# A new hand-out of work: the order table of an attention, DFT and FFN kernel drawn up again

## The chip, the cores and the metric

The kernel runs on one core of a Trainium2 chip. The metric is the device time of one execution in microseconds (us). The engines of the core are TensorE (PE: matmul, with PEld its weight loads), VectorE (DVE), ScalarE (ACT), GpSimd (POOL) and SyncE (SP), which here issues nearly all DMAs. Each engine works through its own list of instructions in order.

## What is computed

Batch 4, sequence 768, 8 heads of 48, so a model width of 384. A linear attention with decay, then a mixing by a two-dimensional DFT (the real part), a normalization, and an FFN of hidden width 1536 with ReLU:

```python
for t in range(S):
    cur = np.einsum('bhd,bhe->bhde', u[None] * kt, vt)
    y[:, :, t] = np.einsum('bhd,bhde->bhe', rt, state + cur)
    state = wt[:, :, :, None] * state + np.einsum('bhd,bhe->bhde', kt, vt)
...
X = np.fft.fft(x, axis=1)
X = np.fft.fft(X, axis=2)
u = x + np.real(X)
un = (u - mean(u)) / np.sqrt(var(u) + 1e-06)
out = u + np.maximum(un @ w_ch1, 0.0) @ w_ch2
```

Inputs and the output are float32.

## The kernel before

**Work.** The sequence of each batch is cut into six chunks of 128 tokens, 24 chunks in all, numbered n = 6 b + c. Names in the rows of the profile are those of the tiles.

*Attention* (`attention2` for pairs of chunks of batch 0, `attention` for the others). A chunk's r, k, v and w are loaded (`in_r` and so on, L587 or L596). ScalarE takes the logarithm of w (`lb`); TensorE sums it along the tokens (L944, L948); ScalarE turns the sums into decays (L950, L963, tile `e`). Products with them are `rkh`: its first half rh (L982, VectorE) and its second half kh (the helper line L533). `rk` is r times k, then times u; its reduction is `dc` (L971), and `vtd` is v times that. rh and kh are transposed to `rkt`: on TensorE for the chunks of batches 0 and 1, and by a DMA transpose (L990) for those of batches 2 and 3. L1014 multiplies the transposed halves, L1019 masks the product (`ah`), L1040 is the state, and L1061 and L1064 give the chunk's output, which L1070 writes to `x`.

*Folding and mixing.* `fold` adds and subtracts mirrored halves of x (`sd`, `xf`; even and odd parts). L1128 is the DFT along the tokens; its results are copied to `hcs`, and a mirrored copy of them to `hcr` (L537, L1138, L1142). L1151 is the DFT along the width; L1153 adds x (`uf`), L1157 and L1159 give mean and variance (`bst`, `agg`), and `un` is normalized up to a scale. `un` is transposed to `unt`: on TensorE (L1174) for batches 0 and 1, by a DMA transpose (L1180) for batches 2 and 3.

*FFN.* A batch is done in two halves of 384 tokens; q counts them from 0 to 7. FFN1 (L1198): twelve results per half, each three matmuls of 128x384, and each evicted with a ReLU from PSUM to `ht` by VectorE (L1203) or ScalarE (L1205). FFN2 (L1216): three blocks of 128 tokens per half. L1220 scales, adds uf (`osb`), and a DMA writes the block out (L1224). The FFN's two weights (`w`, W1 and W2, 1152 KB each) come by DMAs that GpSimd issues (L755).

**Order.** The functions record operations with what they read and write. Several can run on two or three engines: `vec` (L533) on GpSimd or VectorE, `evict` (L556, L557), the FFN1 evictions, `un` and `hcr` on ScalarE or others. `ORDER` (L34) then says everything: for each engine, the numbers of the operations that it does, in order. `schedule` goes through the five lists together. It gives each PSUM tile one of eight banks, in the order in which banks come free by its own planned times; a tile's first operation then depends on the last of the bank's former tile. It also adds one kind of dependence that the data don't ask for:

```python
                    p = port["pool"] if e == "dve" else ahead.end + self.LAT[e] if ahead else 0
...
                if e == "pool" and ahead:
                    o.deps.add(ahead)
            if o.port and e == "dve":
                ahead = o
```

A GpSimd operation that uses the shared port waits for the last such VectorE operation that stands ahead of it in the plan. `emit` turns dependences into semaphore waits, and each engine runs its list in order, so an instruction that waits holds up all that is behind it on its engine, on SyncE too.

Of the kernel before, what the change touches and what calls it, by code (L numbers as in the profile page):

```python
# [32 lines left out]

ORDER = {  # L34
# [24 lines left out]
    "act": (  # L59
# [12 lines left out]
    "dve": (  # L72
# [15 lines left out]
    "pool": (  # L88
# [12 lines left out]
}  # L101


class _Tile:


    __slots__ = ("bank", "ops", "pool", "n_done", "end")

# [1184 lines left out]
```

## Time and profile before

| | |
|---|---|
| Runs | median 183.23 us of 3 (182.76 to 184.08) |
| Profiled execution | 183.38 us, span 181.6 us |
| Outside the span | 1.8 us |
| Busy, us | PE 172.1, DVE 156.6, ACT 120.1, POOL 96.1 |
| Granted TensorE clock | 1.000 |
| First FFN1 matmul | 45.3 us in the chain of waits |
| Last FFN2 matmuls | end about 178.4; then `osb`, and the last output DMA |
| W1's issue | 34.27 us |

"Waited" in a row means that the engine stood idle until the named thing ended. A row of the chain of waits gives the start, the length and what it was; PE rows in it carry a line and how many pieces they hold. Matmuls overlap, so the mean time of one (326 ns for 128x384) is twice their spacing.

### The profile page before, as it was taken

How to read it: one execution, taken by the hardware profiler on the slowest of the kernel's cores; microseconds unless marked ns; L12 is line 12 of the kernel's file. 1: busy time of each engine (PE TensorE's matmuls, PEld its weight loads, DVE VectorE, ACT ScalarE, POOL GpSimd, SP SyncE). 2: the span in 40 equal slices, each digit the busy share in tenths (PEclk: the TensorE clock that was granted, in tenths of full speed). 3: DMA queues.
4: the chain of work that ended last, by engine and by line, in shares of the span. 5: the costliest groups of instructions: out<-in, count | busy, mean ns of one | idle time of the engine just before them, and what ended most of it. 6: DMA issues, size and time to landing. Idle time of an engine off the chain costs nothing.

```text
span 181.6 us, 4639 instructions
## 1 busy us (share of the span) xinstructions
PE 172.1 (95%) x1776; PEld 122.6 (67%) x1776; DVE 156.6 (86%) x372; ACT 120.1 (66%) x286; POOL 96.1 (53%) x121
## 2 busy tenths in 40 slices
PE   5798999999999999999999999997999999999992
PEld 2355577756888767667777776585776866877761
DVE  8999999999996998999999999999688979864233
ACT  4999999999988747678848796349394342415110
POOL 2136988499989806696698035946747230000000
PEclk9999999999999999999999999999999999999999
DMA  5999988999899889898898999999982104330043
GB/s 148 324 323 269 212 168 176 199 187 210 172 191 208 175 158 215 172 221 165 151 196 175 182 222 196 228 198 139 228 194 74 43 4 105 88 110 0 4 167 137
DMA packets 108935, 30.58 MB, mean 168 GB/s; under 512 B 105201, under 2 KB 108402, under 8 KB 108786
## 3 DMA queue, kind: packets, MB, share of 16 engines
q1 hardware_dynamic: 108370, 27.93, 71.8%
q0 software_dynamic: 544, 2.36, 6.9%
q8 instruction: 14, 0.23, 0.5%
q14 instruction: 7, 0.06, 0.1%
HBM read 23.59 MB, written 4.72 MB: 156 GB/s over the span
## 4 chain that ended last, share of the span: by engine, by line
PE 56%; DVE 17%; DMA 6%; SPq 6%; ACT 6%; POOL 5%; issue 2%; DVEq 0%; ACTq 0%; POOLq 0%
PE bank L1216 19%; PE bank L1198 18%; SPq L596 4%; PE bank L1151 4%; DMA rkt<-rkh 3%; PE bank L1128 2%; PE bank L1014 2%; DMA in_k<-in_k_dram 2%; DVE osb L1220 2%; DMA out_dram<-osb 2%; POOL rkh L533 2%; DVE bst L1157 2%; DVE uf L1153 2%; DVE ah L1019 1%; PE bank L839 1%
## 5 line engine op out<-in xcount | busy, mean ns | idle before, releaser
L1198 PE MATMUL bank<-unt,w 128*128 128x384 bf16 x288 | 54.8, 329 | 0.0
L1216 PE MATMUL bank<-w,ht 128*128 128x384 bf16 (+2 forms) x300 | 54.1, 320 | 0.0
L1205 ACT ACTIVATE ht<-bank 128x384 bf16<-128x384 f32 x77 | 35.6, 496 | 26.7 <-PE bank L1198 26.7
L1198 PEld LDWEIGHTS bank<-unt,w 128*128 128x128 bf16 x288 | 38.8, 144 | 6.4 <-DVE ht L1203 0.3
L1216 PEld LDWEIGHTS bank<-w,ht 128*128 128x128 bf16 x300 | 27.7, 98 | 16.0 <-DVE ah L1019 0.2
L1019 DVE TENSOR_TENSOR ah<-bank,msk 128x512 bf16<-128x512 f32 x36 | 23.7, 683 | 2.7 <-PE bank L1014 2.5
L533 POOL TENSOR_TENSOR vtd<-in_v,dc 128x384 f32<-128x384 f32 (+1 forms) x23 | 19.2, 844 | 8.7 <-DVE dc L971 4.8
L533 POOL TENSOR_TENSOR rk<-rk,ub 128x384 f32<-128x384 f32 x21 | 21.1, 1008 | 2.8 <-DVE rkh L533 2.4
L533 POOL TENSOR_TENSOR rkh<-in_k,e 128x384 bf16<-128x384 f32 x16 | 16.0, 1001 | 8.0 <-DMA in_k<-in_k_dram 3.9
L1220 DVE SCALAR_TENSOR_TENSOR osb<-bank,rstd,uf 128x384 f32<-128x384 f32 (+2 forms) x25 | 14.4, 592 | 5.0 <-PE bank L1216 4.5
L533 POOL TENSOR_TENSOR rk<-in_r,in_k 128x384 f32<-128x384 f32 x16 | 16.2, 1019 | 3.5 <-DVE agg L1159 1.7
L1203 DVE TENSOR_SCALAR ht<-bank 128x384 bf16<-128x384 f32 x19 | 10.1, 552 | 7.3 <-PE bank L1198 7.2
L950 ACT ACTIVATE bank<-bank 128x384 f32<-128x384 f32 x18 | 8.8, 494 | 7.7 <-PE bank L944 7.4
L547 ACT ACTIVATE un<-uf,agg 128x384 bf16<-128x384 f32 x18 | 10.8, 616 | 4.4 <-DVE agg L1159 4.2
L1153 DVE TENSOR_TENSOR uf<-bank,x 128x384 f32<-128x384 f32 x24 | 12.7, 548 | 0.7 <-PE bank L1151 0.5
L1157 DVE BATCH_NORM_STATS2 bst<-uf 128x6 f32<-128x384 f32 x24 | 12.7, 548 | 0.1
L547 ACT ACTIVATE lb<-in_w 128x384 bf16<-128x384 f32 (+1 forms) x21 | 12.2, 581 | 0.5 <-DMA in_w<-in_w_dram 0.3
L1070 DVE TENSOR_TENSOR x<-bank,vtd 128x384 f32<-128x384 f32 x18 | 9.8, 549 | 1.6 <-PE bank L1064 1.4
L547 ACT ACTIVATE vb<-in_v 128x384 bf16<-128x384 f32 x21 | 11.1, 534 | 0.0
L556 ACT ACTIVATE rkt<-bank 128x512 bf16<-128x512 bf16 x17 | 10.4, 660 | 0.0
L963 ACT ACTIVATE e<-bank 128x392 f32<-128x392 f32 (+1 forms) x18 | 8.9, 508 | 2.3 <-PE bank L948 2.1
L982 DVE TENSOR_TENSOR rkh<-bank,in_r 128x384 bf16<-128x384 f32 x18 | 9.9, 548 | 0.3 <-ACT bank L950 0.3
(163 smaller groups left out, 346.1 us busy)
## 6 DMA issues: line engine op xcount, KB each, us to landing
out_dram<-osb SPq DMA_DIRECT2D x23, 192.0 KB, 2.4
in_w<-in_w_dram SPq DMA_DIRECT2D x18, 192.0 KB, 4.1
in_k<-in_k_dram SPq DMA_DIRECT2D x18, 192.0 KB, 4.2
in_r<-in_r_dram SPq DMA_DIRECT2D x18, 192.0 KB, 4.0
in_v<-in_v_dram SPq DMA_DIRECT2D x18, 192.0 KB, 4.0
w<-in_moe_w_ch_dram POOLq DMA_DIRECT2D x2, 1152.0 KB, 10.1
in_k<-in_k_dram SPq DMA_DIRECT2D x3, 384.0 KB, 4.8
in_r<-in_r_dram SPq DMA_DIRECT2D x3, 384.0 KB, 4.8
```

The lines of the kernel that those rows point to most:

```text
L533: return lambda e: e.tensor_tensor(out=o, in0=a, in1=b, op=f)
L547: return lambda e: e.activation(o, a, f, **kw)
L556: {"act": lambda e: e.activation(o(), i(), ACTF.Copy), "dve": lambda e: e.tensor_copy(out=o(), in_=i())}, **kw)
L982: op("dve", v_1(DM), lambda e: e.tensor_tensor(out=rh[:, :, 0:D], in0=ps(tce)[:, 0:DM].rearrange("t (h d) -> t h d", d=D), in1=rt[:, :, :] ...
L1019: masked[n] = op("dve", v_1(512), lambda e, x=x: e.tensor_tensor(out=ah[:, x:H:2, :], in0=ps(ta[x])[:, :].rearrange("p (h t) -> p h t", t= ...
L1153: op("dve", v_1(DM), lambda e, kb=kb, t=t: e.tensor_tensor(out=uf[:, kb, :], in0=ps(t)[:, 0:DM], in1=xb[:, kb, 0:DM], op=ALU.add), r=[t, ( ...
L1157: op("dve", v_1(DM), lambda e, kb=kb, bs=bs: e.bn_stats(bs[:, :], uf[:, kb, :]), r=[("UF", i, kb)], w=[("BST", n % 4)])
L1198: ins = e.matmul(ps(t)[:, 0:384], W1[:, m, j:HID:NJ], unt[:, :, m, :], start=(m == 0), stop=(m == NM - 1))
L1203: {"dve": lambda e, j=j, t=t, ht=ht: e.tensor_scalar(out=ht[:, j, :], in0=ps(t)[:, 0:384], scalar1=-1.0, scalar2=0.0, op0=ALU.mult, op1=AL ...
L1205: "act": lambda e, j=j, t=t, ht=ht: e.activation(ht[:, j, :], ps(t)[:, 0:384], ACTF.Relu, scale=-1.0)},
L1216: ins = e.matmul(ps(t)[:, 0:hi - lo], ht[:, j, 128 * x:128 * x + 128], W2[:, j, lo:hi], start=(j == 0), stop=(j == NJ - 1))
L1220: op("dve", v_1(hi - lo) + 64, lambda e, kb=kb, t=t, o=o, lo=lo, hi=hi: e.scalar_tensor_tensor(out=o[:, lo:hi], in0=ps(t)[:, 0:hi - lo], s ...
```

## The change

The operations are the same, and nothing else in the program differs: only the five lists of `ORDER` are replaced. They were drawn up again, with the order and the choice of engine judged by the mean of the planned time over the plan and three variants in which transfers and operations are lengthened by drawn amounts.

```diff
 ORDER = {
     "pe": (
-        "6 1419 1420 1421 1422 1423 1424 1425 86 92 1426 1427 1428 94 78 82 113 97 1429 1430 80 114 146 115 148 128 "
...
+        "6 1419 1420 1421 1422 1423 1424 1425 86 92 1426 94 1427 1428 1429 78 1430 97 1431 82 113 115 146 1432 1433 "
...
```

TensorE keeps its 538 operations and SyncE its 126. ScalarE's go from 286 to 285, VectorE's from 372 to 376, GpSimd's from 117 to 114 (warm-up constants aside). Some 130 operations change engine: 29 from VectorE to ScalarE and 28 back, 26 from GpSimd to VectorE and 21 back, 4 from ScalarE to GpSimd and 2 back. Of the FFN1 evictions 16 go from ScalarE to VectorE and 12 back (ScalarE 77 to 73, VectorE 19 to 23). The twenty warm-up matmuls (L1259) are set among the early work differently, and loads, outputs and DMA transposes stand in another order on SyncE.

Three places. The first is GpSimd around the load of W1 (L755). `xf<-x` is a fold of batch 0, `rkh<-in_k` a kh, `vtd` and `rk` as above. Before:

```order
27 L533 TENSOR_TENSOR vtd<-in_v,dc 128x384
28 L533 TENSOR_TENSOR xf<-x 128x192
29 L533 TENSOR_TENSOR vtd<-in_v,dc 128x384
30 L533 TENSOR_TENSOR rk<-in_r,in_k 128x384 x2
31 L533 TENSOR_TENSOR xf<-x 128x192
32 L755 DMA w<-in_moe_w_ch_dram 128x3x1536
33 L533 TENSOR_TENSOR xf<-x 128x191 x4
34 L533 TENSOR_TENSOR rk<-rk,ub 128x384
35 L1142 COPY hcr<-hcs 128x384
36 L533 TENSOR_TENSOR rkh<-in_k,e_2 128x8x48
37 L533 TENSOR_TENSOR rkh<-in_k,e_0 128x8x48
38 L537 TENSOR_SCALAR hcr<-hcs,cp 128x384
```

And now:

```order
32 L533 TENSOR_TENSOR rkh<-in_k,e_0 128x8x48
33 L533 TENSOR_TENSOR xf<-x 128x192 x2
34 L533 TENSOR_TENSOR xf<-x 128x191
35 L533 TENSOR_TENSOR xf<-x 128x192
36 L533 TENSOR_TENSOR xf<-x 128x191
37 L533 TENSOR_TENSOR xf<-x 128x192
38 L755 DMA w<-in_moe_w_ch_dram 128x3x1536
39 L533 TENSOR_TENSOR rk<-rk,ub 128x384
40 L533 TENSOR_TENSOR rkh<-in_k,e_2 128x8x48
41 L1142 COPY hcr<-hcs 128x384
42 L544 MEMSET xf<- 128x6x66
43 L533 TENSOR_TENSOR rk<-in_r,in_k 128x384
```

The folds that followed the load now stand ahead of it, or have gone to VectorE, and the scaled copy `hcr<-hcs,cp` is no longer on GpSimd here but on ScalarE. Of the folds ahead of the load, the last three (one of chunk 3's even part, one of its odd part, one of chunk 4's even part) wait for VectorE's kh of batch 1 chunk 1.

The second is kh of batch 3 chunk 3, `rkh1<-in_k,e2_0`, with buffer numbers in the names. Before it stood on VectorE, behind the results of FFN2 and the normalization of batch 2:

```order
280 L1220 SCALAR_TENSOR_TENSOR osb0<-bank5,rstd1,uf1 128x384
281 L538 TENSOR_SCALAR un1<-uf0,agg0 128x384
282 L1019 TENSOR_TENSOR ah1<-bank3,msk 128x4x128
283 L538 TENSOR_SCALAR un1<-uf0,agg0 128x384
284 L971 TENSOR_REDUCE dc2<-rk2 128x8
285 L533 TENSOR_TENSOR rkh1<-in_k,e2_0 128x8x48
286 L1048 TENSOR_TENSOR bank6<-bank6,e2_1 128x384
```

Now it is on GpSimd:

```order
95 L533 TENSOR_TENSOR rkh3<-in_k,e2_1 128x8x48
96 L533 TENSOR_TENSOR rk1<-in_r,in_k 128x384
97 L533 TENSOR_TENSOR rk2<-in_r,in_k 128x384
98 L533 TENSOR_TENSOR rkh1<-in_k,e2_0 128x8x48
99 L533 TENSOR_TENSOR vtd2<-in_v,dc0 128x384
100 L533 TENSOR_TENSOR rkh0<-in_k,e2_2 128x8x48
101 L533 TENSOR_TENSOR rk2<-rk2,ub 128x384
```

It stands there between the products of batch 3's chunks 1 to 3 and ahead of the kh of chunk 2 (`rkh0`).

The third is VectorE's end: the evictions of FFN1 (`ht`) and the outputs of FFN2 (`osb`). Before:

```order
311 L538 TENSOR_SCALAR un<-uf,agg 128x384
312 L1203 TENSOR_SCALAR ht<-bank 128x384 x2
313 L1220 SCALAR_TENSOR_TENSOR osb<-bank,rstd,uf 128x384
314 L1203 TENSOR_SCALAR ht<-bank 128x384 x3
315 L1220 SCALAR_TENSOR_TENSOR osb<-bank,rstd,uf 128x384
316 L1203 TENSOR_SCALAR ht<-bank 128x384 x7
317 L1220 SCALAR_TENSOR_TENSOR osb<-bank,rstd,uf 128x384
```

And now:

```order
281 L538 TENSOR_SCALAR un<-uf,agg 128x384
282 L1203 TENSOR_SCALAR ht<-bank 128x384 x3
283 L1220 SCALAR_TENSOR_TENSOR osb<-bank,rstd,uf 128x384 x2
284 L1203 TENSOR_SCALAR ht<-bank 128x384 x7
285 L1220 SCALAR_TENSOR_TENSOR osb<-bank,rstd,uf 128x384
286 L1203 TENSOR_SCALAR ht<-bank 128x384 x5
287 L1220 SCALAR_TENSOR_TENSOR osb<-bank,rstd,uf 128x384
288 L1203 TENSOR_SCALAR ht<-bank 128x384 x2
289 L1220 SCALAR_TENSOR_TENSOR osb<-bank,rstd,uf 128x384 x3
290 L1203 TENSOR_SCALAR ht<-bank 128x384
```

Eighteen of the last 24 evictions stand there instead of twelve; ScalarE has six instead of twelve.

120 rows, old and new, of the table ORDER are left out of this document.

## The prediction

> **What bounds the kernel now.** I read the busy totals first, then the busy time by stretch, then what TensorE waited for, then the chain of waits.
>
> ```profile
> PE 172.1 (95%) x1776; PEld 122.6 (67%) x1776; DVE 156.6 (86%) x372; ACT 120.1 (66%) x286; POOL 96.1 (53%) x121
> ```
>
> The busy time by stretch (columns: from:to, length, then PE, PEld, DVE, ACT and POOL, each with its instructions, then granted clock, DMA share and GB/s):
>
> ```profile
> 20.00:30.00 10.00, 9.95 (x233) 7.30 (x232) 9.97 (x20) 10.00 (x24) 9.35 (x13) 1.00 0.96 199
> 30.00:45.00 15.00, 14.64 (x206) 10.08 (x203) 14.68 (x38) 14.47 (x34) 11.89 (x16) 1.00 1.01 191
> 60.00:75.00 15.00, 15.00 (x146) 10.62 (x145) 13.91 (x28) 9.97 (x27) 7.88 (x9) 1.00 0.91 180
> 105.00:120.00 15.00, 15.00 (x124) 9.62 (x122) 14.51 (x37) 8.33 (x21) 9.97 (x11) 1.00 1.00 209
> 120.00:132.00 12.00, 10.52 (x120) 8.41 (x119) 10.18 (x20) 7.61 (x19) 6.57 (x8) 1.00 1.13 186
> 145.00:160.00 15.00, 15.00 (x99) 10.66 (x96) 12.77 (x32) 5.19 (x11) 1.65 (x2) 1.00 0.32 82
> 160.00:178.50 18.50, 18.39 (x124) 13.11 (x123) 7.29 (x15) 4.42 (x13) 0.00 (x0) 1.00 0.17 60
> ```
>
> Three regimes. Up to 45 us VectorE has no gap (9.97 of 10, 14.68 of 15), and the FFN cannot begin. From 45 us on TensorE is full, except for 1.48 us in 120 to 132. In the last 33 us 0.1 us is lost there, so a wait added there goes straight to the end. The clock is 1.00 throughout. What TensorE waited for, and then the chain of waits at the two places where it lost time (start, length, what; x is the number of pieces):
>
> ```profile
> PE bank L1014 <- DMA rkt<-rkh: 1.7, 2, 1.5
> ```
>
> ```profile
> 33.49 0.48 DVE rk L533
> ...
> 34.27 0.98 POOL w L755
> 35.27 2.01 POOL xf L533 x4
> ...
> 40.81 1.25 POOL hcr L537
> 42.11 0.34 PE bank L1151
> ...
> 45.27 2.50 PE bank L1198 x15
> ...
> 121.78 0.47 DVE rkh L533
> 122.28 5.01 DMA rkt<-rkh
> 127.42 0.40 PE bank L1014 x8
> ```
>
> At 34 us GpSimd issues the load of FFN weight W1. Then it does the last four folds of batch 0 and a mirrored copy (hcr), and the first FFN matmul runs at 45.3. At 122 us one VectorE operation, kh of batch 3 chunk 3 (rkh, L533), comes late; the DMA transpose that reads it lands 5 us later, and TensorE stands for 1.5 us.
>
> **Part 1, the head.** How long W1 takes, and what its issue waited for:
>
> ```profile
> w<-in_moe_w_ch_dram POOLq DMA_DIRECT2D x1, 1152.0 KB, 10.5
> ```
>
> ```profile
> POOL w L755 <- DVE rk L533: 3.0, 1, 3.0
> ```
>
> 34.27 + 10.5 = 44.8, so W1 lands just ahead of the first FFN matmul. The change makes GpSimd wait before W1 for kh of batch 1 chunk 1 rather than for rk of chunk 0. VectorE's list up to that operation is 2.4 us shorter: summed operation by operation at the start-to-start times of the trace (0.47 us for a 384-wide one), 32.0 us become 29.7. The other side is GpSimd's own list. Its prices, where its dense part starts, and what it waited for in that part:
>
> ```profile
> L533 POOL TENSOR_TENSOR rk<-rk,ub 128x384 f32<-128x384 f32 x21 | 21.1, 1008 | 2.8 <-DVE rkh L533 2.4
> L533 POOL TENSOR_TENSOR xf<-x 128x192 bf16<-128x192 f32 x3 | 1.8, 589 | 0.0
> ```
>
> ```profile
> 16.27 0.47 DVE rk L533
> ```
>
> ```profile
> POOL rkh L533 <- ACT rkt L556: 0.9, 1, 0.9
> ...
> POOL rkh L533 <- DVE rk L533: 0.6, 1, 0.6
> ```
>
> Ahead of W1 stand eight folds instead of three, and one wide operation fewer. From VectorE's rk at 16.7, for which the new list waits early, GpSimd has 14.8 us of work to its wait (wide ones about 0.95, folds 0.55 from start to start), which ends at 31.6; VectorE's side, 33.96 - 2.4, gives the same 31.6. Then come three folds, 1.65 us: W1 is issued at about 33.3 and lands at 43.8. The mirrored copy hcr goes from GpSimd to ScalarE:
>
> ```profile
> L1138 ACT ACTIVATE hcr<-hcs 128x384 bf16<-128x384 bf16 x4 | 2.1, 520 | 1.4 <-DVE hcs L557 1.4
> ```
>
> 0.5 us instead of 1.25, so it does not replace W1 as the gate. FFN1 should start near 44.4 instead of 45.3, but in the new order 0.34 us of TensorE's own work has moved from before that point to behind it. Gain: 0.9 - 0.34, taken as **-0.5 us**. Bounds: W1 at 32.7 (a wait that ends 0.6 earlier) gives -1.2. If the two waits of before, 0.9 + 0.6, come back in GpSimd's list, W1 is issued at 34.8 and the head gives 0.5 + 0.34, +0.9.
>
> Both engines move operations with two SBUF inputs across (about 20 each way), and here a row speaks against moving them:
>
> ```profile
> 92.46 0.59 DVE L533 TENSOR_TENSOR vtd<-in_v,dc 128x384 f32<-128x384 f32 x1
> ```
>
> ```profile
> 92.59 1.14 POOL L533 TENSOR_TENSOR vtd<-in_v,dc 128x384 f32<-128x384 f32 x1
> ```
>
> The one clear overlap of such a pair: GpSimd's took 1.14 us. The other GpSimd operations of this kind:
>
> ```profile
> L533 POOL TENSOR_TENSOR vtd<-in_v,dc 128x384 f32<-128x384 f32 x17 | 14.2, 849 | 8.7 <-DVE dc L971 4.8 <-DVE rk L533 2.2 <-DVE agg L1159 1.7
> ```
>
> So 0.3 us lost per meeting. The planner mostly avoids meetings by making GpSimd wait for VectorE (the 3.0 us ahead of W1 is one). The Trainium skill, "SBUF — State Buffer", section "Who interferes with whom", says that a VectorE instruction with two SBUF inputs contends with a GpSimd instruction that reads SBUF, and that the second to issue is blocked until the first ends. The overlap agrees in kind, and by that rule a meeting costs up to the whole of the other operation.
>
> **Part 2, the folds of batch 1 (68 us).** VectorE's list up to the last even fold of batch 1 loses 20 operations and gains 24, by the same prices 63.1 us become 64.2, +1.1 us. The fold in the trace, and the first matmul that reads it:
>
> ```profile
> 66.66 1.02 DVE L533 TENSOR_TENSOR xf<-sd 128x382 bf16<-128x382 f32 x2
> ```
>
> ```profile
> 68.12 0.33 PE L1128 MATMUL bank<-cs,xf 128*128 128x193 bf16 x2
> ```
>
> The fold ends at 67.68, 0.44 us ahead of its use. Afterwards: 67.68 + 1.1 = 68.8, wanted at 68.12 - 0.5 (head) + 0.3 (its new place) = 67.9. A new wait of 0.9 us, so TensorE stands there at **+0.4 us** against before. Bounds: 0, since VectorE also waited about 1 us in 60 to 75 (13.91 of 15) and may catch up, and 1.1.
>
> **Part 3, kh of batch 3 chunk 3.** It moves to GpSimd, ahead of the operations it stood behind. GpSimd has the room:
>
> ```profile
> 124.24 2.40 POOL L533 TENSOR_TENSOR vtd<-in_v,dc 128x384 f32<-128x384 f32 x3 [4.06 <-DVE dc L971]
> ```
>
> There it takes 1.0 us instead of 0.55. The transpose's other operand is ready early, so its issue moves from 122.28 to what SyncE's queue and that operand allow:
>
> ```profile
> 118.42 0.53 DVE L982 TENSOR_TENSOR rkh<-bank,in_r 128x384 bf16<-128x384 f32 x1
> ```
>
> 119 to 120 us, landing by 125. TensorE wants it at about 126, and the 1.5 us wait goes: **-1.5 us**, from +0.4 to -1.1. Next in line are the transposes of batch 3 chunk 5, issued at 133.80:
>
> ```profile
> rkt<-rkh SPq DMA_TRANSPOSE x1, 5.1
> ```
>
> ```profile
> 139.03 0.40 PE bank L1014 x8
> ```
>
> 133.80 + 5.1 = 138.9, used 0.13 us later. VectorE's list up to their last operand is 1.8 us shorter (123.1 to 121.3), but they are wanted 0.7 us of TensorE's work earlier (each matmul of 384 columns counted at a third of 0.49, the row below), so the kernel can be at most 1.1 us ahead there. That caps the sum at the same -1.1. Bounds for the part: 0 and -1.5.
>
> **Part 4, the tail.** FFN1's results leave PSUM by ScalarE or VectorE. Of the last 24 evictions VectorE does 18 instead of 12.
>
> ```profile
> 158.73 1.49 DVE L1203 TENSOR_SCALAR ht<-bank 128x384 bf16<-128x384 f32 x3
> ```
>
> ```profile
> 168.46 0.49 PE bank L1198 x3
> ```
>
> ```profile
> L1220 DVE SCALAR_TENSOR_TENSOR osb<-bank,rstd,uf 128x384 f32<-128x384 f32 x23 | 13.7, 607 | 1.0 <-DMA out_dram<-osb 0.4 <-PE bank L1216 0.4
> ```
>
> Three evictions in a row take 1.49 us, 0.47 each from start to start; TensorE makes a result in 0.49. Over the first 21 results (10.3 us) VectorE has 15 evictions and 3 outputs of 0.55 from start to start: 15 x 0.47 + 3 x 0.55 = 8.7 us. It fits by 1.6 us, and bank by bank I find each free some 0.3 us before TensorE needs it. **0 us**; bounds 0 and +3 (the second rival). The last output operation and its DMA are the same instructions as before.
>
> **Sum.** -0.5 + 0.9 - 1.5 + 0 = -1.1 us on the profiled 183.38: 182.3. The median of the runs shown, 183.23, stands 0.15 below the profiled time, so I say **182.2 us**. Its own range, 181.2 to 183.2, has the sum between -2.0 (VectorE makes up 0.9 us before 139) and 0 (the other bound of part 3).
>
> **Rivals.** *All waits fall.* VectorE makes up its 1.1 us before 68 us, and the transposes follow: head -1.2, fold 0, kh -1.5 give -2.7: 183.2 - 2.7 = 180.5. For it: VectorE's own waits of 1 us there. Against it: the 0.13 us margin at 139.
>
> *The tail's banks.* ScalarE's new list puts the eviction of one late result ahead of two earlier ones, and VectorE's leaves one early result to the end of its run: three of the eight banks are held. Beyond the 0.3 us of cover each of the six results made meanwhile costs TensorE one eviction of 0.55: +3.3, and 183.2 - 1.1 + 3.3 = 185.4. It decides if VectorE reaches its run of seven evictions over 0.3 us late. For it: TensorE has no idle time to absorb it (18.39 of 18.5), and VectorE's 11.2 us of idle time in that stretch lies mostly near its end. Against it: the sum above fits.
>
> *The meetings.* If GpSimd's folds ahead of W1 meet VectorE's four at 0.3 us each, W1 comes 1.2 us later and the sum is +0.1: 183.3. By the rule of the Trainium skill, "SBUF — State Buffer", named above, a meeting could cost a whole fold, 0.6 us, four times: 184.5; the traced pair speaks for the smaller price, and that version has 0.03 of this rival's chance.
>
> **Chances.** Forecast 0.38, of which 0.10 lies below 181.4. All waits fall: 0.22. Tail: 0.22. Meetings: 0.11. Something that I have not named, slower: 0.07. A measurement of this kernel can tell about 1% (1.8 us) from no change, so the borders are 181.4 and 185.1. Faster 0.10 + 0.22 = 0.32; within 1% 0.28 + 0.11 = 0.39; slower 0.22 + 0.07 = 0.29. The range 180.3 to 186.0 leaves out the best end of the first rival (0.08) and the worse end of the tail and the unnamed (0.12).
>
> **What would show it.** Head: W1's issue at 33 to 33.6, and the first FFN1 matmul near 44.4; an issue after 35 refutes it. Folds: TensorE waiting up to 0.9 us at 67 to 69 for xf. Kh: the wait for rkt gone, and the next one, if any, at about 138 for chunk 5. Tail: busy share near 1 from 154 us on; VectorE's evictions named as what TensorE waits for there would show the second rival. A new wait of over 1 us between 70 and 120 us would mean that I missed the place that decides.

## The result and the profile after

| | before | after |
|---|---|---|
| Runs side by side, median us | 183.15 of 17 (182.43 to 184.22) | 182.17 of 17 (181.49 to 183.61) |
| Ratio, 95% interval | | 0.9946 (0.9924 to 0.9968) |
| Profiled execution, span, us | 183.38, 181.6 | 181.62, 179.8 |

The changed order is 0.5% faster, 1.0 us by the medians, 1.8 us between the two profiled executions. An execution whose mean granted clock was 0.98 to 0.99 instead of 1.00 took 0.7 to 1.9 us longer in each kernel that had both, and some kernels below had more of these than the changed one with its 2 of 17. The page's line of busy time shows TensorE's work unchanged and a smaller span around it:

```profile
PE 171.9 (96%) x1776; PEld 123.8 (69%) x1776; DVE 158.4 (88%) x376; ACT 121.3 (67%) x285; POOL 95.1 (53%) x118
```

The busy time by stretch, columns as before:

```profile
30.00:45.00 15.00, 14.79 (x205) 11.16 (x205) 14.92 (x37) 14.63 (x33) 12.73 (x17) 1.00 0.99 186
60.00:75.00 15.00, 14.94 (x147) 10.56 (x146) 14.22 (x30) 8.80 (x23) 9.22 (x10) 1.00 0.92 178
120.00:132.00 12.00, 12.00 (x133) 9.43 (x132) 10.78 (x22) 9.66 (x25) 7.61 (x9) 1.00 0.97 176
132.00:145.00 13.00, 11.81 (x118) 8.78 (x117) 11.40 (x23) 7.13 (x20) 4.91 (x6) 1.00 0.53 95
145.00:160.00 15.00, 15.00 (x94) 10.87 (x93) 13.30 (x34) 2.77 (x6) 1.45 (x2) 1.00 0.28 67
160.00:176.50 16.50, 16.50 (x115) 11.75 (x113) 8.86 (x18) 2.90 (x9) 0.00 (x0) 1.00 0.25 92
```

The stretch that lost 1.48 us before (120 to 132) is full now; the next one (132 to 145) lacks 1.19. Before, that one had this row:

```profile
132.00:145.00 13.00, 12.86 (x124) 9.58 (x122) 11.53 (x22) 7.39 (x21) 6.57 (x7) 1.00 0.44 103
```

From 145 us on nothing is lost. What TensorE waited for in 132 to 145 in the changed kernel (us in total, how often, the longest):

```profile
PE bank L1014 <- DMA rkt<-rkh: 1.2, 1, 1.2
```

That is the name of the wait that was to go, at another chunk. The chain of waits in the head, at the folds of batch 1, and at this wait (SPq is SyncE's DMA queue):

```profile
44.55 3.46 PE bank L1198 x21
...
66.46 0.56 DVE sd L533
67.02 0.48 DVE xf L533
67.54 1.69 PE bank L1128 x18
...
124.47 0.50 ACT e L963
124.96 0.39 ACT ht L1205
125.35 1.42 SPq L1180
126.81 0.72 SPq L596
127.58 3.53 DMA in_k<-in_k_dram
131.20 0.89 DVE rkh L533
132.12 4.60 DMA rkt<-rkh
136.81 0.40 PE bank L1014 x8
```

FFN1 begins at 44.55 (45.27 before). Before, TensorE had also stood 0.3 us for the mirrored copy `hcr`, just ahead of FFN1; no such row is left:

```profile
PE bank L1151 <- POOL hcr L537: 0.3, 1, 0.3
```

At 67.5 the last fold on VectorE now ends just ahead of the DFT matmul that reads it. At 136.8 TensorE has waited for the DMA transposes of batch 3 chunk 5, whose kh (`rkh`, L533) ended at 132.09. GpSimd's timeline (start, length, what, and in brackets the idle time ahead of it) has W1's issue:

```profile
31.96 1.70 POOL L533 TENSOR_TENSOR xf<-x 128x192 bf16<-128x192 f32 x3 [0.49 <-DVE rkh L533]
33.59 1.00 POOL L755 DMA_DIRECT2D w<-in_moe_w_ch_dram  x1
```

To see where the time came from, I priced each matmul at its spacing and subtracted, at equal amounts of TensorE's own work, that work from the time on the clock. What is left is the time TensorE has lost so far. How the short matmuls are priced moves the difference at 60 between about -0.1 and -0.4, that at 76 between about -0.4 and -0.65, and the others less:

| TensorE's work done, us | lost before | lost after | difference | what lies between |
|---|---|---|---|---|
| 44 | 9.87 | 9.32 | -0.55 | the head |
| 60 | 10.00 | 9.75 | -0.25 | folds of batch 1 |
| 76 | 10.45 | 10.07 | -0.38 | |
| 88 | 11.24 | 10.27 | -0.97 | batch 2, chunks 3 to 5 |
| 112 | 11.54 | 10.47 | -1.07 | |
| 116 | 13.20 | 10.54 | -2.66 | kh of batch 3 chunk 3 |
| 128 | 13.72 | 12.24 | -1.48 | the wait for chunk 5 |
| 152 | 14.03 | 12.36 | -1.67 | the tail |

So the new order was 2.7 us ahead at chunk 3 and gave 1.2 of it back at chunk 5. The experiments ask whether that wait is a ceiling, as I had predicted, and whether it can be taken away.

### The profile page after: what moved, and what is told of

Same layout as the page of the kernel before. It is cut to its first block, busy times and chain, and to the rows that moved or that the text cites. A ratio compares the mean times of both kernels' runs of the same rounds, so it can differ in the third digit from the quotient of the medians.

```text
span 179.8 us, 4644 instructions
## 1 busy us (share of the span) xinstructions
PE 171.9 (96%) x1776; PEld 123.8 (69%) x1776; DVE 158.4 (88%) x376; ACT 121.3 (67%) x285; POOL 95.1 (53%) x118
## 4 chain that ended last, share of the span: by engine, by line
PE 79%; DVE 6%; ACT 6%; DMA 5%; SPq 1%; issue 1%; ACTq 0%; DVEq 0%
PE bank L1198 24%; PE bank L1216 23%; PE bank L1151 5%; PE bank L1128 4%; PE bank L1014 3%; DMA rkt<-rkh 3%; DMA in_k<-in_k_dram 2%; PE bank L948 2%; PE bank L1064 2%; PE bank L913 1%; PE bank L839 1%; PE bank L944 1%; PE bank L1061 1%; PE bank L862 1%; PE bank L1040 1%; PE bank L1174 1%
## 5 line engine op out<-in xcount | busy, mean ns | idle before, releaser
L1205 ACT ACTIVATE ht<-bank 128x384 bf16<-128x384 f32 x73 | 33.4, 497 | 22.7 <-PE bank L1198 21.9
L1019 DVE TENSOR_TENSOR ah<-bank,msk 128x512 bf16<-128x512 f32 x36 | 23.2, 680 | 2.0 <-PE bank L1014 1.9
L533 POOL TENSOR_TENSOR rk<-rk,ub 128x384 f32<-128x384 f32 x18 | 18.0, 1005 | 9.8 <-DVE rk L533 8.4
L533 POOL TENSOR_TENSOR vtd<-in_v,dc 128x384 f32<-128x384 f32 (+1 forms) x22 | 18.2, 832 | 6.7 <-DVE bank L1048 2.9
L533 POOL TENSOR_TENSOR rk<-in_r,in_k 128x384 f32<-128x384 f32 x16 | 16.3, 1020 | 9.9 <-DVE xf L533 7.8
L533 POOL TENSOR_TENSOR rkh<-in_k,e 128x384 bf16<-128x384 f32 x18 | 18.0, 1003 | 5.5 <-ACT e L963 4.8
L547 ACT ACTIVATE un<-uf,agg 128x384 bf16<-128x384 f32 x20 | 11.8, 617 | 12.9 <-DVE agg L1159 12.8
L1203 DVE TENSOR_SCALAR ht<-bank 128x384 bf16<-128x384 f32 x23 | 11.7, 552 | 4.3 <-PE bank L1198 4.2
L547 ACT ACTIVATE vb<-in_v 128x384 bf16<-128x384 f32 x24 | 12.1, 519 | 2.7 <-DMA in_v<-in_v_dram 2.7
L556 ACT ACTIVATE rkt<-bank 128x512 bf16<-128x512 bf16 x20 | 12.1, 652 | 0.1
L1151 PE MATMUL bank<-dtm,hcr 128*128 128x384 bf16 x36 | 9.6, 326 | 0.1
```

The source lines that it names most:

```text
L533: return lambda e: e.tensor_tensor(out=o, in0=a, in1=b, op=f)
L547: return lambda e: e.activation(o, a, f, **kw)
L556: {"act": lambda e: e.activation(o(), i(), ACTF.Copy), "dve": lambda e: e.tensor_copy(out=o(), in_=i())}, **kw)
L1019: masked[n] = op("dve", v_1(512), lambda e, x=x: e.tensor_tensor(out=ah[:, x:H:2, :], in0=ps(ta[x])[:, :].rearrange("p (h t) -> p h t", t= ...
L1151: return e.matmul(ps(t)[:, 0:DM], (hcs if kb < NP else HCR)[:, j, a:a + 128], DTM[:, j, :], start=(j == 0), stop=(j == 2))
L1203: {"dve": lambda e, j=j, t=t, ht=ht: e.tensor_scalar(out=ht[:, j, :], in0=ps(t)[:, 0:384], scalar1=-1.0, scalar2=0.0, op0=ALU.mult, op1=AL ...
```

## The experiments

Each edit moves operations in the order table and nothing else (`schedule` then gives banks and added dependences anew); the rows stand in the diffs in the words of the table's operations. Ratios are to the kernel before, run on the same chip. The changed kernel's own is 0.9946.

### Kh alone, in the order of before

In the kernel before, kh of batch 3 chunk 3 goes from VectorE to GpSimd, and SyncE issues its transposes ahead of a load.

```diff
 VectorE
 L971 TENSOR_REDUCE dc<-rk 128x8
-L533 TENSOR_TENSOR rkh<-in_k,e_0 128x8x48
 GpSimd
 L533 TENSOR_TENSOR vtd<-in_v,dc 128x384
+L533 TENSOR_TENSOR rkh<-in_k,e_0 128x8x48
 SyncE
-L990 DMA_TRANSPOSE rkt<-rkh 128x8x128
+L990 DMA_TRANSPOSE rkt<-rkh 128x8x128 x2
 L596 DMA in_w<-in_w_dram 128x8x48
-L990 DMA_TRANSPOSE rkt<-rkh 128x8x128
```

> The kernel before with part 3 of the change alone: kh of batch 3 chunk 3 goes from VectorE to GpSimd, after vtd of chunk 0, and the load of w of chunk 5 stands behind that chunk's transpose on SyncE instead of ahead of it. Theory (waits in series, capped at chunk 5's transpose, which had 0.13 us of margin at 139.0): the wait at 127 falls from 1.5 to 0.4 or less, a wait of about 1.1 appears at 138, time 183.0, ratio 0.999. Rival (the wait counts in full): no new wait, 182.0, ratio 0.994.

Measured: 182.20 us, ratio 0.9970 (0.9944 to 0.9997). The wait at chunk 3 halves, from 1.66 to 0.83 by the table's method, and its rest is no longer kh; the ratio lies between theory and rival. In the chain of waits of this kernel the two transposes and the load stand in a row on SyncE:

```profile
120.35 1.22 SPq L990
121.61 1.32 SPq L990
122.98 4.34 DMA in_w<-in_w_dram
127.34 0.53 ACT lb L547
```

At chunk 5 no wait came back (TensorE reaches it at 138.35 instead of 139.03, and the whole wait for `rkt` is 0.2 us): the transposes were issued 0.5 us earlier (133.3 for 133.8) and flew 4.0 us instead of 5.1. A ceiling at chunk 5 with its 0.13 us of margin would have let nothing through unless they too came earlier; they did, by 0.5 us of issue, which fits VectorE's list being one operation shorter ahead of them, and by 1.1 us of flight. One of the 110 moves between engines thus gives 0.3% (0.8 us by the medians), against 0.5% (1.0 us) for the whole table; the intervals overlap, so these runs do not show that the other moves are worth anything together.

### The new order without the kh move

The reverse, in the changed kernel: kh of chunk 3 back on VectorE, its transposes behind two loads.

```diff
 GpSimd
-L533 TENSOR_TENSOR rkh<-in_k,e_0 128x8x48
 L533 TENSOR_TENSOR vtd<-in_v,dc 128x384
 VectorE
 L1220 SCALAR_TENSOR_TENSOR osb<-bank,rstd,uf 128x384
+L533 TENSOR_TENSOR rkh<-in_k,e_0 128x8x48
 SyncE
-L990 DMA_TRANSPOSE rkt<-rkh 128x8x128 x2
+L990 DMA_TRANSPOSE rkt<-rkh 128x8x128
 L596 DMA in_v<-in_v_dram 128x8x48
 L596 DMA in_k<-in_k_dram 128x8x48
+L990 DMA_TRANSPOSE rkt<-rkh 128x8x128
```

> The changed kernel with part 3 undone: kh of batch 3 chunk 3 back on VectorE, after the output of block 3 of batch 1, and its transpose behind the loads of v of chunk 3 and k of chunk 4 on SyncE. Theory (series and cap): a wait of 1.0 to 1.7 us comes back at 126, the wait of 1.35 for chunk 5 at 137 goes down to 0.3 or less, time 182.4, ratio 0.996. Rival (the move of kh carries its 1.5 us to the end): both waits stand, 183.6, ratio 1.002.

Measured: 184.50 us, ratio 1.0086 (1.0050 to 1.0121): 2.3 us above the changed kernel by the medians, 1.7 by the profiles. At a mean granted clock of 0.996 or more the medians are 183.81 and 182.08, also 1.7 apart. The same move was worth 0.8 us in the order of before. TensorE's timeline has the old wait back at chunk 3:

```profile
126.97 0.62 PE L1014 MATMUL bank<-rkt 48*128 48x128 bf16 x16 [1.84 <-DMA rkt<-rkh]
...
131.58 0.32 PE L948 MATMUL bank<-lb,nle 128*128 128x384 bf16 x1
```

The wait at chunk 5 should have absorbed 1.2 us of this, if it were a ceiling; it is still there, 1.0 us long (the profile names a ScalarE operation for it, but the transposes landed at 138.4, 0.1 us ahead of its end). The second row says why. L948 sums chunk 5's logarithms; in the changed kernel it stands at 129.64:

```profile
129.64 0.32 PE L948 MATMUL bank<-lb,nle 128*128 128x384 bf16 x1
```

It is 1.94 us later here, just as L1014 of chunk 3 is (126.97 for 125.03), since it stands behind it in TensorE's own list. Chunk 5's decay, its rh and kh, and its transposes follow from it. So the landing for chunk 5 moves with chunk 3, and the two waits add up.

### W1 earlier, and W1 later

W1's load ahead of the last three folds, and in another kernel one wide operation later.

```diff
 GpSimd (earlier)
 L533 TENSOR_TENSOR xf<-x 128x191
+L755 DMA w<-in_moe_w_ch_dram 128x3x1536
 L533 TENSOR_TENSOR xf<-x 128x192
 L533 TENSOR_TENSOR xf<-x 128x191
 L533 TENSOR_TENSOR xf<-x 128x192
-L755 DMA w<-in_moe_w_ch_dram 128x3x1536
 GpSimd (later)
-L755 DMA w<-in_moe_w_ch_dram 128x3x1536
 L533 TENSOR_TENSOR rk<-rk,ub 128x384
+L755 DMA w<-in_moe_w_ch_dram 128x3x1536
```

> The changed kernel with the load of W1 ahead of GpSimd's last three folds instead of behind them. W1 is then issued at about 32.0 instead of 33.6 and lands near 42.6; the folds end 1 us later, at 34.7. Theory (besides W1, the folds and the chain from them through un gate the first FFN1 matmul): it starts at 44.4 to 45.2 instead of 44.55. Rival (W1 alone gates it): it starts at 44.2 or earlier, as far as un allows. Either way the wait for chunk 5 takes up the difference: time within 0.4 us of the changed kernel, ratio 0.993 to 0.997.

> The changed kernel with the load of W1 one operation later in GpSimd's list, behind the product rk with u of batch 1 chunk 0, which waits for VectorE until 36.1: W1 is issued at 37.1 instead of 33.6, lands near 47.7, and the first FFN1 matmul cannot run before that, 3.3 us later than in the changed kernel's trace. Theory (what TensorE loses in the head stays lost, since nothing behind has slack but chunk 5's wait, which gives back 0.3): about 3.0 us, 185.2, ratio 1.011. Rival (behind the head VectorE sets the pace and TensorE catches up): at most half, 183.7, ratio 1.003.

Earlier: 182.51 us, ratio 0.9979 (0.9952 to 1.0006); the interval overlaps that of the changed kernel. W1 is issued at 32.19, 1.4 us sooner, but flies 12.0 us instead of 10.6 and lands at 44.2, as in the changed kernel. FFN1 begins at 45.40, 0.85 later. What TensorE waited for:

```profile
PE bank L1014 <- DMA rkt<-rkh: 0.9, 1, 0.9
...
PE bank L1125 <- POOL xf L533: 0.6, 1, 0.6
```

The load's issue takes 1.00 us of GpSimd, so the folds of batch 0 behind it are late for the DFT (L1125). So the folds gate FFN1 here, by way of the DFT and the normalization behind them, and W1's landing does not. In the changed kernel that landing is only 0.4 us ahead of FFN1, so W1 has little room either. Of the 0.9 us lost in the head, chunk 5's wait gives back 0.3 (0.9 for 1.2).

Later: 184.94 us, four executions, ratio 1.0136 (1.0081 to 1.0190). The wide operation waits 2.45 us for VectorE, and W1 waits with it, until 37.05, 3.5 us later:

```profile
36.12 0.99 POOL L533 TENSOR_TENSOR rk<-rk,ub 128x384 f32<-128x384 f32 x1 [2.45 <-DVE rk L533]
37.05 1.00 POOL L755 DMA_DIRECT2D w<-in_moe_w_ch_dram  x1
```

TensorE then waits for W1 by name:

```profile
47.32 2.95 PE L1198 MATMUL bank<-unt,w 128*128 128x384 bf16 x17 [2.06 <-DMA w<-in_moe_w_ch_dram]
```

The table's method gives 2.9 us lost in the head and 3.2 at the end: the head is in series with everything behind it, and W1 does gate it once it is late.

### The loads for chunk 5 ahead of the transposes

The chain of the changed kernel leads to chunk 5 by the load of its k. So SyncE issues the loads of w and k before the transposes of chunks 2 and 3, and r before those of `un`.

```diff
 SyncE
+L596 DMA in_w<-in_w_dram 128x8x48
+L596 DMA in_k<-in_k_dram 128x8x48
 L990 DMA_TRANSPOSE rkt<-rkh 128x8x128 x2
 L596 DMA in_v<-in_v_dram 128x8x48
 L596 DMA in_k<-in_k_dram 128x8x48
-L596 DMA in_w<-in_w_dram 128x8x48
+L596 DMA in_r<-in_r_dram 128x8x48
 L1180 DMA_TRANSPOSE unt<-un 128x9x128
-L596 DMA in_r<-in_r_dram 128x8x48
-L596 DMA in_k<-in_k_dram 128x8x48
```

> The changed kernel with three loads moved on SyncE's list alone: w and k of batch 3 chunk 5 stand ahead of the transposes of chunks 2 and 3 instead of behind them, r of chunk 5 ahead of the transpose of un. In the changed kernel's trace TensorE's one long wait after the head, 1.35 us at 136.8, is for the transpose of chunk 5, whose operand kh waited for k to land at 131.1. Theory (the sum is capped by that transpose): kh then waits for its decay e at 130.5 instead, the transpose is issued about 1 us earlier, the wait falls from 1.35 to 0.2 to 0.5, and nothing behind takes it back: about 181.2 us, ratio to the kernel before 0.989. Rival (the next DMA transpose, of un of batch 3, landed 0.1 us before its use and caps the sum again): the wait moves to 153, about 182.1, ratio 0.994.

Measured: 183.26 us, ratio 1.0018 (0.9992 to 1.0044), slower than the changed kernel. TensorE's timeline shows two waits where there was one:

```profile
127.75 0.62 PE L1014 MATMUL bank<-rkt 48*128 48x128 bf16 x16 [1.08 <-DMA rkt<-rkh]
...
139.30 0.40 PE L1014 MATMUL bank<-rkt 48*128 48x128 bf16 x8 [1.06 <-DMA rkt<-rkh]
```

SyncE's queue has the cause; the transposes stand behind two more loads, and their own issue, 2.6 us for the two in the changed kernel, takes longer as well:

```profile
119.71 1.53 SPq L596 DMA_DIRECT2D in_k<-in_k_dram  x1
121.34 3.17 SPq L990 DMA_TRANSPOSE rkt<-rkh  x2
```

Chunk 3's land at 127.6 instead of 123.6. Of these 4.0 us, 1.1 were lost in the head, where nothing had been changed: there the granted clock of this execution was 0.50 for 3.4 us from 9.9 us on. Between 10 and 12 us TensorE did 10 matmuls at this clock, and 26 at 1.00 in the changed kernel. The other 2.9 are the loads', and chunk 3 had 1.4 to spare.

### The loads in an idle slot

SyncE is idle at 112 us. There r and k of chunk 5 go, ahead of an earlier transpose of `un`; in a second kernel w goes there too.

```diff
 SyncE
 L1224 DMA out_dram<-osb 128x384
 L596 DMA in_r<-in_r_dram 128x8x48
+L596 DMA in_r<-in_r_dram 128x8x48
+L596 DMA in_k<-in_k_dram 128x8x48
 L1180 DMA_TRANSPOSE unt<-un 128x9x128
...
 L1180 DMA_TRANSPOSE unt<-un 128x9x128
-L596 DMA in_r<-in_r_dram 128x8x48
-L596 DMA in_k<-in_k_dram 128x8x48
```

> The changed kernel with the loads of r and k of batch 3 chunk 5 moved to where SyncE stood idle, behind the load of r of chunk 3 (111.7 to 113.7 us in its trace), far ahead of the transposes of chunks 2 and 3. Theory (chunk 5's wait came from its k landing late, and the failed edit before lost its gain by putting loads right in front of those two transposes): kh of chunk 5 then waits for its decay only, its transpose is issued 0.5 us earlier, the wait at 137 falls from 1.35 to 0.8 or less, no new wait for chunks 2 and 3: 0.5 us below the changed kernel, 181.6, ratio 0.992. Rival (the transposes lose whatever the loads gain, wherever these stand): waits of 0.5 to 1 us for chunks 2 and 3, 182.5 or more, ratio 0.998.

> The same with the load of w of chunk 5 there as well. The decay of chunk 5 hangs on TensorE's order more than on this load, so the theory gives little besides what SyncE's list and the DMA engines gain at 123 to 127: 181.4 to 181.7, ratio 0.991 to 0.993. Rival (three loads in a row ahead of the transpose of un make that one late, at 117 to 118): a wait of about 1 us at 118, 182.8, ratio 1.000.

With r and k: 182.47 us, ratio 1.0006 (0.9967 to 1.0045), no gain. k landed at 116.4, 15 us early, and VectorE still does kh at the same time:

```profile
130.83 0.55 DVE L982 TENSOR_TENSOR rkh<-bank,in_r 128x384 bf16<-128x384 f32 x1
131.29 0.97 DVE L533 TENSOR_TENSOR rkh<-in_k,e 128x384 bf16<-128x384 f32 x1
```

The chain of waits had named the load because it ended last (131.1), 0.1 us after the rh ahead of kh. Take it away, and rh and the decay it needs (130.36 to 130.85 on ScalarE) stand there. This execution was 0.4 us later than the changed kernel's already in the head, which the edit does not touch, and its wait for chunk 5 was 1.0 us instead of 1.2, so the load may be worth 0.2 us or so; the runs show none of it. With w as well: 183.65 us, ratio 1.0042 (1.0010 to 1.0073); the transpose of `un` is now behind three loads, and TensorE waits for it:

```profile
PE bank L1198 <- DMA unt<-un: 1.0, 1, 1.0
```

### Kh of chunk 5 on GpSimd

If VectorE's list sets chunk 5, its kh should leave VectorE. It goes to GpSimd, with the load of k in the idle slot.

```diff
 VectorE
 L982 TENSOR_TENSOR rkh<-bank,in_r 128x8x48
-L533 TENSOR_TENSOR rkh<-in_k,e_2 128x8x48
 L533 TENSOR_TENSOR sd<-x 128x385
 GpSimd
 L533 TENSOR_TENSOR rk<-rk,ub 128x384
+L533 TENSOR_TENSOR rkh<-in_k,e_2 128x8x48
 L533 TENSOR_TENSOR sd<-x 128x385
```

> The changed order with two operations of batch 3 chunk 5 moved: kh goes from VectorE (131.2 to 132.1 us) to GpSimd, behind the wide product that ends at 130.7, and the load of k goes into SyncE's idle slot at about 112 us, so that k is there. Theory (waits add; chunk 5's landing is set by VectorE's list, in which kh stands behind rh): both operands are ready at about 131.7 instead of 132.1, and VectorE's list behind it is 0.9 us shorter. The wait for chunk 5's transposes falls from 1.2 to 0.8 or less, and the time is 0.4 us below the changed kernel, ratio to the kernel before 0.990 to 0.995. Rival (the next stage gives it back: the odd difference of chunk 4 on GpSimd, which stands behind kh now, comes 1 us later, and what reads it waits): the wait for the transposes falls the same, a wait of up to 0.6 us for x or xf appears between 133 and 143 us, and the ratio is 0.995 to 1.000.

Measured: 182.62 us, ratio 0.9997 (0.9969 to 1.0024). The wait for chunk 5's transposes is gone, and one of 1.4 us stands just ahead of it:

```profile
PE bank L1040 <- ACT vb L547: 1.4, 1, 1.4
```

VectorE's timeline tells where it comes from:

```profile
132.77 1.36 DVE L533 TENSOR_TENSOR sd<-x 128x385 f32<-128x385 f32 x1 [1.62 <-POOL sd L533]
134.16 0.56 DVE L533 TENSOR_TENSOR xf<-sd 128x384 bf16<-128x384 f32 x1
134.64 0.56 DVE L1048 TENSOR_TENSOR bank<-bank,e 128x384 f32<-128x384 f32 x1
```

The difference `sd` on GpSimd comes 1 us later behind kh, VectorE waits 1.62 for it, the state's decay (L1048) ends at 135.20 instead of 133.64, and TensorE's state matmul (L1040) waits for that by way of ScalarE. The rival was right, though I had put the wait at x or xf. Nor were the transposes much earlier: issued at 131.8 for 132.1, they landed at 136.5 for 136.7, so some 0.8 us of their wait was only covered by the new one.

### Parts of the new order with the rest of the old

To give the head its own price, the new lists were used up to 44.5 us and the old ones after (and up to 104 us), each also with the kh move above. The lists are cut at a time:

```diff
 ORDER = {
-    (each engine's list of before)
+    (the new list up to the cut, then what is left, in the order of before)
```

> The new order up to the first FFN1 matmul (all that the changed kernel's trace starts before 44.5 us), then the kernel before's order for all the rest. Theory (TensorE's waits add up in series): the head's gain of 0.4 to 0.5 us in the traces reaches the end: 182.5, ratio 0.997. Rival (VectorE, dense up to 120 us, sets the pace behind the head, and a lead of TensorE is lost by 68 us): 183.0, ratio 1.000.

> The same head, with kh of batch 3 chunk 3 on GpSimd and its transpose ahead of the load of w of chunk 5 besides (the edit of the run before that measured 0.8 us). Theory (series): 0.45 + 0.8 = 1.25 us ahead of the kernel before, 181.75, ratio 0.993, below the changed kernel. Rival (they overlap): 182.2, ratio 0.997.

> The new order up to 104 us of the changed kernel's trace, then the kernel before's order, with kh of batch 3 chunk 3 late on VectorE as there. Theory (series): the 0.9 us that TensorE is ahead at this point in the traces reach the end: 182.1, ratio 0.995; the wait of 1.5 us for the transpose of chunk 3 is there. Rival (that transpose's time is set by VectorE's list, which is no shorter): the wait grows by what TensorE is ahead, 182.9, ratio 0.9995.

> The same up to 104 us, then the kernel before's order with kh of batch 3 chunk 3 on GpSimd. Theory (series): 0.9 + 0.8 = 1.7 us ahead of the kernel before, 181.3, ratio 0.991: the changed kernel without its new wait for chunk 5 at 137. Rival (chunk 5's transpose caps the sum at the changed kernel's): a wait of about 1 us at 137 and 182.2, ratio 0.995.

Ratios: 1.0105 (1.0081 to 1.0129) and 1.0134 (1.0091 to 1.0176) for the cut at 44.5, 1.0241 (1.0192 to 1.0290) and 1.0232 (1.0196 to 1.0268) for that at 104. All four are slower than either whole order, and theory and rival missed alike. The two kernels cut at 104 share one wait behind the seam, at 110.6 and 110.9 us:

```profile
PE bank L1040 <- DVE vb L979: 2.9, 1, 2.9
```

Their ratios are not this wait alone, since nearly all their executions had a lower granted clock: the one at 1.00 took 185.19 us, against 182.61 for the kernel before at that clock, 2.6 us more.

The one cut at 44.5 without the kh move waits 0.6 us in three pieces at 45 to 51 us and 1.4 at 98.6, far behind its seam:

```profile
98.56 0.40 PE L1014 MATMUL bank<-rkt 48*128 48x128 bf16 x8 [1.44 <-ACT lb L547]
```

An order is a whole: what each engine has done by the cut differs, and the other list relies on it. The head's own gain can't be had this way and rests on the traces and the two W1 kernels.

## Why the prediction came out right

The time was predicted as 182.2 and measured as 182.17; the sum of -1.1 us stands beside -1.0 by the medians and -1.8 by the profiles. That the two times agree to 0.03 us is luck. In the profiles the fold cost 0.6 us less than its term, 0.8 us was gained where the sum has nothing, and 1.2 us was lost to a wait that the sum counts only as a ceiling. Point by point:

- **Head, -0.5:** -0.55 at 44 us of work. W1 was issued at 33.59 (33.3 predicted), and FFN1 began at 44.55 (44.4). The size is right, but W1 was not the gate that the prediction took it for. By issue and flight it landed at 44.8 before and at 44.2 after, 0.5 and 0.4 us ahead of FFN1, and TensorE did not wait for it in either trace. W1's issue stands in the chain of before because GpSimd's folds and `hcr` are behind it in the list; the prediction compared the lengths of the two copies, and did not see that `hcr` on GpSimd was what TensorE waited for (0.3 us). No run says what the rest of the gain comes from. After, the chain goes from the DFT over the normalization to FFN1. The size is no better than a few tenths: the other seven kept traces with the same head lost 0.0 to 1.2 us more in it (the 1.2 is the one with the low clock), and the second trace with the old head 0.2 more than the first, so some 0.4 us is a fairer figure.
- **Folds of batch 1, +0.9 (which took the sum to +0.4):** +0.30 (-0.55 to -0.25), with TensorE waiting 0.23 us at 67.54 and less around it. The operation is the one that was named and the size lies between the stated bounds of 0 and 1.1, but it is a third of the term: the fold ended at 67.50, not 68.8.
- **Kh of chunk 3, -1.5:** -1.59 (-1.07 to -2.66). The transposes were issued at 120.2 and landed at 123.6, 1.4 us ahead of their use.
- **"That caps the sum":** the place was right, the wait at 136.8 for chunk 5; the size and the meaning were not. Chunk 5's wait took back 1.18 us of the 2.66 gained until then, where the sum, standing at its cap, foresaw no wait. The cap of 1.1 us came out as 1.5: used at 136.81 instead of 139.03, 2.2 earlier, less the 0.7 by which it was wanted earlier. The issue moved by 1.7 (1.8 predicted), and the flight fell from 5.1 to 4.6, which I had held constant. And the wait is no ceiling on what part 3 is worth: without the kh move the profile is 1.7 us longer, not the 0.5 that a fixed landing would leave (1.7 less the wait of 1.2), because chunk 5's decay stands behind chunk 3 on TensorE. What failed is thus the step from "next in line" to a fixed time.
- **Tail, 0:** no time lost from 145 us on, so the rival of the tail's banks is out.
- **The range:** its upper end, 183.2, is given as part 3 at its bound of 0; that bound makes the sum +0.4 and the time 183.6. It did not matter here.
- **What I missed:** 0.8 us gained between 60 and 112 us of work, 0.6 of it between 76 and 88, where in the old order the transposes of batch 2 landed just before their use. One of the small waits is in TensorE's timeline of before:

```profile
96.49 0.40 PE L1014 MATMUL bank<-rkt 48*128 48x128 bf16 x8 [0.18 <-DMA rkt<-rkh]
```

It is read off the traces; no run undid it alone, and how much of it is left after chunk 5's wait stays open. So does most of the 0.8 us by which the two profiled executions differ more than the medians; some 0.2 of it is the head above, and single executions of one kernel spread over 2 us.

The rival of all waits falling (-2.7) is out: the small margin at chunk 5 was the argument against it, and 1.2 us came back there. The rival of the meetings was not what happened in the head, where W1 came 0.3 us later than predicted, not 1.2. No kernel tried was faster than the changed one.

## What to carry to other kernels

Price a wait by following what stands behind it in the lists of all engines: if the next late transfer is itself started by work behind the first wait, the two add up, and only work that is independent of it sets a ceiling. The last link in a chain of waits may be a tie: the load that ended last here was 0.1 us behind the operation next to it, and taking it away gained nothing. An operation can stand in the chain of waits only because others are behind it in its engine's list: W1's issue did, and its landing held nothing up. In an order table in which every engine is nearly full, a moved load or a moved operation pays where it lands, so judge it by what it is put in front of.

## What the runs showed of the hardware

DMA transposes of the same size flew for between 3.1 and 5.2 us from issue to landing (batch 3, chunks 2 to 5): in the changed kernel 3.4 us for chunk 3 and 4.6 for chunk 5. Their issue on SyncE, 1.23 us when alone, took up to 3 us close behind loads, though no run separates the loads from what else was in flight; this row of SyncE's queue is from the kernel without the kh move, where loads were issued 0.95 and 1.57 us before it:

```profile
121.81 2.96 SPq L990 DMA_TRANSPOSE rkt<-rkh  x1
```

Kh of chunk 5 took 0.89 us on VectorE, where such an operation takes 0.55, while GpSimd was at work on two SBUF operands; the row of GpSimd's timeline in the changed kernel:

```profile
130.66 1.02 POOL L533 TENSOR_TENSOR sd<-x 128x385 f32<-128x385 f32 x1
```

GpSimd's ended at 131.68, and kh, begun at 131.20, at 132.09. The Trainium skill, "SBUF — State Buffer", section "Who interferes with whom", has the second of such a pair blocked until the first ends: by that rule kh would have run from 131.68 to 132.23. The measured end is 0.14 us earlier, so here the rule is nearly right, and a meeting costs about the overlap, 0.34 of 0.48 us, and not a whole operation. Three like pairs in other kernels also ended 0.12 to 0.14 us ahead of the rule: `kh` of chunk 5 without the kh move (133.54) and with r and k in the idle slot (132.26), and `sd` with kh of chunk 5 on GpSimd (134.13).

The granted clock of TensorE fell to 0.50 for 3.41 us in two kept traces: that with the loads ahead of the transposes, from 9.9 us, and that cut at 104 us without the kh move, from 111.7 us, 1.1 us after a wait of 2.94 us had ended. The other kernel cut at 104 had a wait of 2.95 us and no such stretch, so the wait alone does not decide it; what does is open. One such stretch in 182 us makes a mean of 0.991, which is the figure of most executions below 0.996.
